# First weight piece of an LN-MLP kernel moved to ACT's DMA queue, and three more filling products

## The chip, the cores and the metric

One core of one Trainium2 chip. The time is the device time of one execution in microseconds (us). Three runs of the kernel before gave 396.5, 396.9 and 397.19 us; the median is 396.9.

## The reference

```
y = _layernorm(x, axis=-1)                                    # x: 1 x 2048 x 1024, no scale or shift
h = gelu(einsum("bsd,df->bsf", y, w1) + b1, approximate=True) # w1: 1024 x 3584
return einsum("bsf,fd->bsd", h, w2) + b2                      # w2: 3584 x 1024
```

All tensors are bf16.

## The kernel before, in words

The 2048 rows of x are cut into 16 tiles of 128 rows (tile 0 to tile 15), and these into 4 blocks of 512. For each block the first GEMM makes h (28 rows of 128 features, each a sum over 8 slices `dt` of the 1024 inputs), ACT applies bias and gelu from PSUM, and the second GEMM makes the output, to which DVE adds b2. The instruction order of each engine is written out by hand: every operation is put on a list of its engine (`sp`, `pe`, `act`, `dve`, `pool`) with the names of the events it waits for, and the lists are emitted in that order. Every load of the kernel before is on SP's list.

The opening is about block 0, where x and w1 are still on their way. What the prediction's steps touch:

- **Loads** (`dma`, L185 to 186; `LOADS`, L32; issued at L208 to 226). SP issues x tile 0 (x0), x tile 1 (x1), then w1 in pieces: c0, c1, c2, then b1, c3, c4, x tile 2 (x2), c5 and so on. A piece cN of the first sixteen is one slice `dt` of w1 for 8 rows: 128 x 1024 bf16, 256 KB, as large as an x tile. c0 to c3 are dt 0 to 3 of rows 0 to 7, c4 to c7 the same dt of rows 8 to 15, c8 to c15 dt 4 to 7 of the same rows; c16 and on serve rows 16 to 23 and the last ones.
- **Filling products** (`fill`, L295; called at L542 and L544). A matmul of ones into a bank that is overwritten later. Nine of 512 columns stand at the head of PE's list; then come two transposes of tile 0, two filling products of 128 columns, and two transposes of tile 1.
- **Centring.** For tiles 0 and 1 ACT and DVE each sum a part of the row (L431 and L434), DVE subtracts the mean (L440, result in c_sb), PE transposes slices of c_sb against an identity matrix (`pe_T`, L311), and ACT copies the transposed slices to yT_sb (L317). Scaling by 1/std comes later, on the products (below).
- **The order of products** (`OPEN`, L23; `pe_cell`, L339): slice 0 with c0 for tile 0 (8 products of 128 columns), four transposes, slice 0 with c0 for tile 1 (8 more), then slices 1 to 3 with c1 to c3 for both tiles (8 products of 256 columns for each piece), then c4 to c7, c8 to c15, c16 and on. Two rows share a PSUM bank (a unit). The eight banks are full after unit 7, so unit 8 (row 16) needs bank 0 and unit 9 (row 18) needs bank 1 again; each is free when ACT's gelus of that bank's first unit are done (L380).
- **What frees those banks.** After x2 has landed, DVE takes its mean (L478), moves slices of tiles 0 and 1 (L494), normalises and transposes tile 2 (L484, L487), spreads the factors 1/std (L519 to L530), and multiplies the products of the first units by them (L370). ACT's gelus of these units (L380) come behind that.

SP and PE list, as code:

```
LOADS = (0, 1, 2, "b1", 3, 4, -2, 5, 6, 7, 8, 9, 10, -3) + tuple(range(11, 22))
...
        fill(N_FILL_A, TPB)
        pe_T(0, GROUPS[0][0], c_sb[:, 0, :])
        fill(N_FILL_C, 1)
        pe_t[0] = T_PE_START
```

Of the kernel before, what the change touches and what calls it, by code (L numbers as in the profile page):

```python
# [11 lines left out]
P = 128  # L12
TB = 512
TPB = TB // P
# [2 lines left out]
UGROUPS = ((0, 4), (4, 8), (8, 10), (10, 11), (11, 12))  # L17
NPAIR = 2 * UGROUPS[-1][1]
NCEN = 2
N_FILL_A = 9  # L20
N_FILL_C = 2
JT = 4
OPEN = (("T", 1, 0), (0, 0, 1, 0, 1), ("T", 0, 1), ("T", 1, 1), (0, 1, 2, 0, 1), (0, 0, 2, 1, JT), (1, 0, 2, 0, JT),  # L23
        (0, 0, 2, JT, 8), (1, 0, 2, JT, 8), (2, 0, 2, 0, 8), (3, 0, 2, 0, 8), (4, 0, 2, 0, 8))
# [4 lines left out]
          ((0, 2, 6), (2, JT, 4)))  # L29
ACT_BLOCKS_01 = ((0, 1), (0, 2), (1, 2), (1, 3))  # L30
ACT_BLOCKS = ((0, 1), (0, 2), (0, 3), (1, 2), (1, 3), (2, 3))
LOADS = (0, 1, 2, "b1", 3, 4, -2, 5, 6, 7, 8, 9, 10, -3) + tuple(range(11, 22))  # L32
NOB = 2
TAIL_CUTS = (0, 384, 512)
N_W2_CHUNKS = 2
# [58 lines left out]
def bass_standalone__mixer_channel_mlp__prompt_kernel(  # L94
# [46 lines left out]
    w1v = w1.rearrange("(t p) f -> p t f", p=P)  # L141
    w2v = w2.rearrange("(t p) d -> p t d", p=P)

    with ExitStack() as es:
        sb = lambda name, shape, dt: es.enter_context(nc.sbuf_tensor(name, shape, dt))

        w1_sb = sb("w1_sb", [P, DT, F], BF16)
# [22 lines left out]
        ps = es.enter_context(nc.psum_tensor("ps", [P, NBANK, 512], F32))  # L170
        psb = ps[:, :, :].bitcast(BF16)
        one = nc.const_aps.tensor(1.0, [P, P], BF16)

        sp = _Prog(None)
        pe = _Prog("s_pe")
        act = _Prog("s_act")
# [8 lines left out]
        def dma(dst, src, sig, nbytes, q=None):  # L185
            (q or sp).op(lambda e, dst=dst, src=src: e.dma_start(dst, src), sig=sig, sem="d_" + sig, inc=16)  # L186
            dma_bytes[0] += nbytes
            est[sig] = DMA_T0 + dma_bytes[0] / DMA_BYTES_PER_US

        def load_x_tile(i, q=None):  # L190
            dma(x_sb[:, i, :], xf[i * P:(i + 1) * P, :], f"x{i}", P * D * 2, q)
            x_ev[i] = f"x{i}"
# [4 lines left out]
            for i in range(b0 * TPB, b1 * TPB):  # L197
                x_ev[i] = f"xb{b0}"

        def load_w1(ci):  # L200
            j0, j1, a, b = w1_chunks[ci]
            dma(w1_sb[:, j0:j1, a:b], w1v[:, j0:j1, a:b], f"w1c{ci}", (j1 - j0) * P * (b - a) * 2)

        def load_w2(ci):
            dma(w2_sb[:, ci * W2C:(ci + 1) * W2C, :], w2v[:, ci * W2C:(ci + 1) * W2C, :], f"w2c{ci}",
# [2 lines left out]
        for i in range(2):  # L208
            load_x_tile(i)
        for o in LOADS:  # L210
            if o == "b1":
                sp.op(None, waits=["b1z"])
                dma(b1r_sb[0:FT, :], b1.rearrange("(t p) -> t p", p=P), "b1", F * 2)
            elif o < 0:
                load_x_tile(-o)
            else:
                load_w1(o)
        assert n_open == 1 + max(o for o in LOADS if o != "b1")
        for ci in range(n_open, len(w1_chunks)):
            load_w1(ci)  # L220
# [4 lines left out]
        if NB > 2:  # L225
# [4 lines left out]
                sig="ident")  # L230
# [61 lines left out]
        bank_read = {}  # L292
        pe_t = [T_PE_START]

        def fill(n, k):  # L295
            rhs = one.unsqueeze(1).broadcast_to([P, k, P])
            for _ in range(n):
                pe.op(lambda e: e.matmul(ps[:, 0, 0:k * P], lhsT=one, rhs=rhs, start=True, stop=True))  # L298

        def pe_T(i, group, src):  # L300
            blk, t = divmod(i, TPB)
            j0, j1, bank = group
            bap = psb[:, bank, :]
            evs = yT_ev.setdefault(i, [None] * DT)
            for j in range(j0, j1):
                waits = []
                if j == j0:
                    waits = ["ident"] + ([bank_read[bank]] if bank in bank_read else [])
                if j == j0 or y_ev[i][j] != y_ev[i][j - 1]:
                    waits.append(y_ev[i][j])  # L310
                pe.op(lambda e, j=j, o=(j - j0) * P: e.transpose(  # L311
                    out=bap[:, o:o + P], in_=src[:, j * P:(j + 1) * P], identity=ident[:, :]),
                    waits=waits, sig=(f"tp{i}_{j0}" if j == j1 - 1 else None))
                evs[j] = f"te{i}_{j0}"
            psrc = bap[:, 0:(j1 - j0) * P].rearrange("p (j s) -> p j s", j=j1 - j0)
            dst = yT_sb[:, blk % 2, j0:j1, t * P:(t + 1) * P]
            act.op(lambda e, dst=dst, psrc=psrc: e.copy(out=dst, in_=psrc), waits=[f"tp{i}_{j0}"], sig=f"te{i}_{j0}")  # L317
            bank_read[bank] = f"te{i}_{j0}"
            pe_t[0] += (j1 - j0) * 0.056
# [106 lines left out]
            store_last[(ob, region)] = sev  # L426

        act.op(lambda e: e.preload_act_table(ACT.Gelu_apprx_tanh))
        def sums(i, na):
            n2 = (D - na) // 2  # L430
            act.op(lambda e: e.activation(out=hT_sb[:, 2 * NRAW + i, 0:na], in_=x_sb[:, i, 0:na], func=ACT.Copy,  # L431
                                          scale=1.0 / D, accum_out=sum_sb[:, 2 * i:2 * i + 1]),
                   waits=[f"x{i}"], sig=f"sa{i}")
            return (lambda e: e.tensor_tensor_reduce(out=o_sb[:, i, 0:n2], in0=x_sb[:, i, na:na + n2],  # L434
                                                     in1=x_sb[:, i, na + n2:D], op0=ALU.add, op1=ALU.add,
                                                     scale=1.0 / D, scalar=0.0, accum_out=sum_sb[:, 2 * i + 1:2 * i + 2]),
                    [f"x{i}"], f"sd{i}")

        def centre(i, j0, j1):
# [4 lines left out]
            y_ev.setdefault(i, []).extend([f"y{i}_{j0}"] * (j1 - j0))  # L444

        sd = [sums(0, SA0), sums(1, HC)]
        def turn_half(i):
            dve_put((lambda e: e.transpose(out=hT_sb[:, NPAIR - 4 + i, :], in_=c_sb[:, i, JT * P:D]), y_ev[i][JT:DT],
# [10 lines left out]
        for i in range(NCEN):  # L459
            pool.op(lambda e, i=i: e.tensor_tensor(out=tot_sb[:, i:i + 1], in0=sum_sb[:, 2 * i:2 * i + 1],  # L460
                                                   in1=sum_sb[:, 2 * i + 1:2 * i + 2], op=ALU.add),
                    waits=[f"sa{i}", f"sd{i}"], sig=f"tot{i}")
# [60 lines left out]
        for q in range(4):  # L523
            f = q ^ 1
# [3 lines left out]
        for h in range(2):  # L528
            f = h ^ 1
# [7 lines left out]
        for k, (tq, q) in enumerate(joint):  # L537
            if k == 4:
                dve_put(op_rm_pair(N_RM_EARLY - 1, N_RM_EARLY - 1))
            move(dve, 2, 2, tq, q)  # L540

        fill(N_FILL_A, TPB)  # L542
        pe_T(0, GROUPS[0][0], c_sb[:, 0, :])
        fill(N_FILL_C, 1)  # L544
        pe_t[0] = T_PE_START

# [80 lines left out]
        ci = fi = 0  # L627
        while ci < len(crit) or fi < len(fills):
            take_crit = fi >= len(fills)
            if not take_crit and ci < len(crit):  # L630
                rel_f, _, blk_f = fills[fi]
                if crit[ci][0] <= max(t_dve, rel_f) + CRIT_SLACK and blk_f > crit[ci][2]:
                    take_crit = True
            if take_crit:
                rdy, o, _ = crit[ci]
                ci += 1
            else:
                rdy, o, _ = fills[fi]
# [46 lines left out]
```

## Time and profile before

| | before |
|---|---|
| three runs, us | 396.5, 396.9, 397.19 (median 396.9) |
| the profiled execution, us | 396.88 |
| span of its instructions, us | 395.6 |
| PE busy | 392.7 us of the span, 99% |
| PE from 0 to 5 us, and from 5 to 10 us | busy 4.17 and 4.77 us |
| DMA, first 30 us | 342 GB/s on the mean |
| granted TensorE clock over the span | 1.0 |

The span begins with the first instruction and ends with the last; 1.28 us of the profiled execution's time lie outside it. In a row of the timeline the columns are the start in us, the length in us, the engine, the line, the operation, what it writes and reads, how many instructions are merged in the row, and in brackets the idle time of the engine before it and what ended that. PE is TensorE's matmul, PEld its weight load (each matmul has one), SPq is SP issuing a DMA. Matmul records overlap, since a record runs to the end of the pipeline; the distance from start to start is the rate. A DMA has landed when all its parts have been reported to its semaphore.

### The profile page before, as it was taken

Reading aid. Unit: us, or ns where it says so; the run is one execution under the profiler, and the core shown is the slowest. Engines: PE = TensorE matmul, PEld = TensorE weight load, DVE = VectorE, ACT = ScalarE, POOL = GpSimd, SP = SyncE. Lnnn points to the kernel's source line nnn. Section 1 sums busy time; section 2 is a strip of 40 time slices with the busy share of each in tenths; the row PEclk is TensorE's granted clock in tenths of the full one; section 3 lists DMA queues with packets and bytes.
Section 4 is the critical chain, followed back from the end, with each engine's and each line's share of the span. In section 5 each row is a group of like instructions: output and inputs, shape, how many; then the busy total and the mean of one; then the engine's idle time right before and its main releaser. Section 6 shows DMA issues by size and latency. Waiting matters only on the chain.

```text
span 395.6 us, 4775 instructions
## 1 busy us (share of the span) xinstructions
PE 392.7 (99%) x2039; PEld 197.6 (50%) x2039; DVE 155.6 (39%) x344; ACT 94.4 (24%) x169; POOL 10.8 (3%) x31
## 2 busy tenths in 40 slices
PE   8999999999999999999999999999999999999998
PEld 5888844444444444444444444444444444444445
DVE  5998989989996005987100000001100000001011
ACT  6787520000144332000023443100003334400000
POOL 1202000110002000000000000000000000000000
DMA  8999940000000000000000000000000000000000
GB/s 284 377 366 384 386 148 22 17 29 13 27 2 0 0 2 0 29 23 17 28 13 0 2 0 0 15 13 27 25 16 15 0 0 2 0 13 28 13 27 28
DMA packets 16190, 23.64 MB, mean 60 GB/s; under 512 B 1194, under 2 KB 8362, under 8 KB 16170
## 3 DMA queue, kind: packets, MB, share of 16 engines
q1 hardware_dynamic: 16170, 23.34, 16.7%
q8 instruction: 16, 0.26, 0.3%
q14 instruction: 4, 0.03, 0.0%
HBM read 19.14 MB, written 4.19 MB: 59 GB/s over the span
## 4 chain that ended last, share of the span: by engine, by line
PE 98%; DMA 1%; SPq 0%; DVE 0%; issue 0%
PE ps L408 49%; PE ps L339 49%; DMA w_sb<-in_w_dram 1%; SPq L186 0%; DVE o_sb L419 0%
## 5 line engine op out<-in xcount | busy, mean ns | idle before, releaser
L339 PE MATMUL ps<-yT_sb,w_sb 128*128 128x512 bf16 (+2 forms) x1096 | 195.0, 340 | 0.1
L408 PE MATMUL ps<-w_sb,hT_sb 128*128 128x512 bf16 (+2 forms) x924 | 194.1, 373 | 0.0
L339 PEld LDWEIGHTS ps<-yT_sb,w_sb 128*128 128x128 bf16 x1096 | 106.3, 98 | 87.8 <-DMA w_sb<-in_w_dram 0.3
L408 PEld LDWEIGHTS ps<-w_sb,hT_sb 128*128 128x128 bf16 x924 | 89.3, 98 | 104.5
L359 ACT ACTIVATE hT_sb<-ps,b_sb 128x512 bf16<-128x512 f32 x88 | 60.5, 688 | 236.3 <-PE ps L339 231.9
L419 DVE TENSOR_TENSOR o_sb<-ps,b_sb 128x512 bf16<-128x512 f32 (+2 forms) x33 | 22.3, 675 | 198.3 <-PE ps L408 198.3
L284 DVE STREAM_TRANSPOSE yT_sb<-x_sb 32x256 bf16<-32x256 bf16 x192 | 83.7, 436 | 28.8 <-PE ps L339 25.8
L380 ACT ACTIVATE hT_sb<-ps,b_sb 128x256 bf16<-128x256 f32 x48 | 18.8, 507 | 8.6 <-PE ps L339 7.3
L237 DVE BATCH_NORM_STATS2 st_sb<-x_sb 128x6 f32<-128x512 bf16 x24 | 15.8, 667 | 0.1
L242 POOL TENSOR_TENSOR rstd_sb<-mv_sb,nhalf 128x1 f32<-128x1 f32 x12 | 6.6, 548 | 100.4 <-DVE mv_sb L245 100.4
L252 DVE TENSOR_SCALAR x_sb<-x_sb,mv_sb,rstd_sb 128x1024 bf16<-128x1024 bf16 x12 | 6.6, 546 | 3.0 <-POOL rstd_sb L242 2.0
L370 DVE TENSOR_TENSOR ps<-ps,rbc_sb 128x512 f32<-128x512 f32 x12 | 7.5, 693 | 0.1
L503 ACT COPY yT_sb<-o_sb 32x256 bf16<-32x256 bf16 x12 | 4.8, 402 | 3.1 <-DVE o_sb L487 2.9
L298 PE MATMUL ps<-const-bfloat16-1.0 128*128 128x512 bf16 (+1 forms) x11 | 4.4, 568 | 0.8 <-PEq L670 0.8
L245 DVE BATCH_NORM_AGGREGATE mv_sb<-st_sb 128x2 f32<-128x15 f32 x12 | 2.7, 223 | 1.2
L503 DVE COPY yT_sb<-o_sb 32x512 bf16<-32x512 bf16 x10 | 2.8, 284 | 0.2
L298 PEld LDWEIGHTS ps<-const-bfloat16-1.0 128*128 128x128 bf16 x11 | 1.4, 139 | 2.7 <-issue 2.7
L494 DVE COPY yT_sb<-hT_sb 32x256 bf16<-32x256 bf16 x12 | 2.6, 218 | 0.1
L487 DVE STREAM_TRANSPOSE o_sb<-c_sb 128x1024 bf16<-128x1024 bf16 x2 | 2.5, 1245 | 0.1
L466 ACT ACTIVATE hT_sb<-x_sb,sum_sb 128x1024 bf16<-128x1024 bf16 x2 | 2.3, 1148 | 0.6 <-DVE sum_sb L478 0.6
L466 ACT ACTIVATE hT_sb<-x_sb,tot_sb 128x1024 bf16<-128x1024 bf16 x2 | 2.3, 1146 | 0.0
L434 DVE CUSTOM_DVE_ANT_0 o_sb<-x_sb 128x384 bf16<-128x384 bf16 (+1 forms) x2 | 1.0, 488 | 3.3 <-DMA x_sb<-in_x_dram 3.3
(33 smaller groups left out, 23.4 us busy)
## 6 DMA issues: line engine op xcount, KB each, us to landing
w_sb<-in_w_dram SPq DMA_DIRECT2D x2, 3584.0 KB, 22.2
w_sb<-in_w_dram SPq DMA_DIRECT2D x18, 256.0 KB, 5.7
out_dram<-o_sb SPq DMA_DIRECT2D x31, 128.0 KB, 1.7
x_sb<-in_x_dram SPq DMA_DIRECT2D x1, 2048.0 KB, 17.1
w_sb<-in_w_dram SPq DMA_DIRECT2D x3, 512.0 KB, 9.9
x_sb<-in_x_dram SPq DMA_DIRECT2D x4, 256.0 KB, 4.0
w_sb<-in_w_dram SPq DMA_DIRECT2D x1, 1024.0 KB, 10.2
x_sb<-in_x_dram SPq DMA_DIRECT2D x1, 1024.0 KB, 11.4
```

Of the source, the lines that this page charges most:

```text
L237: return (lambda e, i=i, h=h: e.bn_stats(st_sb[:, i, 6 * h:6 * (h + 1)], x_sb[:, i, h * HC:(h + 1) * HC]), [x_ev.get(i, f"x{i}_{h}")], f"s ...
L242: pool.op(lambda e, i=i, to=to: e.tensor_tensor(out=to[:, i:i + 1], in0=mv_sb[:, i, 1:2], in1=nhalf[:, i:i + 1], op=ALU.pow), waits=[f"mv{ ...
L252: return (lambda e, i=i: e.tensor_scalar(out=x_sb[:, i, :], in0=x_sb[:, i, :], scalar1=mv_sb[:, i, 0:1], scalar2=rstd_sb[:, i:i + 1], op0= ...
L284: res.append((lambda e, src=src, dst=dst: e.transpose(out=dst, in_=src), waits, (f"tr{i}" if lastop else None), 0.47))
L298: pe.op(lambda e: e.matmul(ps[:, 0, 0:k * P], lhsT=one, rhs=rhs, start=True, stop=True))
L339: pe.op(lambda e, dt=dt: e.matmul(ps[:, bank, o0:o0 + n1 - n0], lhsT=w1_sb[:, dt, r * P:(r + 1) * P], rhs=yT_sb[:, b % 2, dt, n0:n1], star ...
L359: act.op(lambda e, r=r, bank=bank: e.activation(out=hT_sb[:, r, :], in_=ps[:, bank, :], func=ACT.Gelu_apprx_tanh, bias=b1_sb[:, r:r + 1], ...
L370: return (lambda e: e.tensor_tensor(out=pv, in0=pv, in1=rv, op=ALU.mult), [f"mp0_{u}", "rbc"], f"rmp_{u}", 0.70)
L380: act.op(lambda e, r=r, k=k: e.activation(out=hT_sb[:, r, half * NC:(half + 1) * NC], in_=ps[:, bank, k * NC:(k + 1) * NC], func=ACT.Gelu_ ...
L408: pe.op(lambda e, st=st, ft=ft, c0=c0, c1=c1, bank=bank: e.matmul(ps[:, bank, 0:c1 - c0], lhsT=hT_sb[:, ft, st * P:(st + 1) * P], rhs=w2_s ...
L419: crit.append((est[sig], (lambda e, ob=ob, c0=c0, c1=c1, bank=bank: e.tensor_tensor(out=o_sb[:, ob, c0:c1], in0=ps[:, bank, 0:c1 - c0], in ...
L503: op = (lambda e: e.tensor_copy(out=dst, in_=src)) if eng is dve else (lambda e: e.copy(out=dst, in_=src))
```

## The change

c0 is taken off SP's list. ACT issues it on its own DMA queue, after it has loaded its function table and has waited until the fourth of the nine filling products is done; on ACT's list this stands ahead of the sums of tiles 0 and 1. The nine filling products are issued in the same place as before (4 and 5, the fourth now signals). The filling products between tile 0's and tile 1's transposes are five instead of two. Nothing else moves: PE's, DVE's and POOL's lists are otherwise the same, and SP's list is the same without c0.

```diff
-N_FILL_A = 9
-N_FILL_C = 2
+N_FILL_A = (4, 5)
+N_FILL_C = 5
...
-LOADS = (0, 1, 2, "b1", 3, 4, -2, 5, 6, 7, 8, 9, 10, -3) + tuple(range(11, 22))
+ACT_LOADS = (0,)
+LOADS = (1, 2, "b1", 3, 4, -2, 5, 6, 7, 8, 9, 10, -3) + tuple(range(11, 22))
...
-        def load_w1(ci):
+        def load_w1(ci, q=None):
             j0, j1, a, b = w1_chunks[ci]
-            dma(w1_sb[:, j0:j1, a:b], w1v[:, j0:j1, a:b], f"w1c{ci}", (j1 - j0) * P * (b - a) * 2)
+            dma(w1_sb[:, j0:j1, a:b], w1v[:, j0:j1, a:b], f"w1c{ci}", (j1 - j0) * P * (b - a) * 2, q)
...
-        def fill(n, k):
+        def fill(n, k, sig=None):
             rhs = one.unsqueeze(1).broadcast_to([P, k, P])
-            for _ in range(n):
-                pe.op(lambda e: e.matmul(ps[:, 0, 0:k * P], lhsT=one, rhs=rhs, start=True, stop=True))
+            for i in range(n):
+                pe.op(lambda e: e.matmul(ps[:, 0, 0:k * P], lhsT=one, rhs=rhs, start=True, stop=True),
+                      sig=sig if i == n - 1 else None)
...
         act.op(lambda e: e.preload_act_table(ACT.Gelu_apprx_tanh))
+        act.op(None, waits=["fill"])
+        for ci in ACT_LOADS:
+            load_w1(ci, act)
...
-        fill(N_FILL_A, TPB)
+        fill(N_FILL_A[0], TPB, "fill")
+        fill(N_FILL_A[1], TPB)
         pe_T(0, GROUPS[0][0], c_sb[:, 0, :])
         fill(N_FILL_C, 1)
```

## The prediction, as put on record before the changed kernel ran

> **What bounds the kernel now.** I read the page first: PE is the bound, and the change can only move the few microseconds in which PE is not.
>
> ```profile
> PE 392.7 (99%) x2039; PEld 197.6 (50%) x2039; DVE 155.6 (39%) x344; ACT 94.4 (24%) x169; POOL 10.8 (3%) x31
> ```
>
> Then the chain that ended last, over the first 20 us. From 6.95 us on it is matmuls alone; ahead of them stands one load, whose issue began at 2.16 and which landed at 6.91. That is c1, SP's fourth.
>
> ```profile
> 2.16 4.75 DMA w_sb<-in_w_dram
> 6.91 0.04 issue
> 6.95 13.09 PE ps L339 x118
> ```
>
> Third, the timeline of the weight loads from 4.1 to 7.2 us, because their brackets name what PE waited for.
>
> ```profile
> 4.45 0.32 PEld L311 LDWEIGHTS ps<-ident,c_sb 128*128 128x128 bf16 x2 [0.53 <-POOL tot_sb L460]
> 4.72 0.25 PEld L298 LDWEIGHTS ps<-const-bfloat16-1.0 128*128 128x128 bf16 x2
> 5.39 0.11 PEld L311 LDWEIGHTS ps<-ident,c_sb 128*128 128x128 bf16 x2 [0.41 <-DVE c_sb L440]
> 5.56 0.46 PEld L339 LDWEIGHTS ps<-yT_sb,w_sb 128*128 128x128 bf16 x8
> 5.98 0.27 PEld L311 LDWEIGHTS ps<-ident,c_sb 128*128 128x128 bf16 x4
> 6.20 0.49 PEld L339 LDWEIGHTS ps<-yT_sb,w_sb 128*128 128x128 bf16 x8
> 6.95 0.33 PEld L339 LDWEIGHTS ps<-yT_sb,w_sb 128*128 128x128 bf16 x4 [0.26 <-DMA w_sb<-in_w_dram]
> ```
>
> The transposes of tile 1 wait for its centring until 5.39. The first product's weights load at 5.56, its matmul starts at 5.59. The 16 small products and 4 transposes end at 6.70; then PE stands for 0.25 us until c1 is there.
>
> Last I looked for the next place where PE stands. There is one, near 20.4 us, and its cause is not a load:
>
> ```profile
> 20.42 0.66 PEld L339 LDWEIGHTS ps<-yT_sb,w_sb 128*128 128x128 bf16 x7 [0.23 <-ACT hT_sb L380]
> ```
>
> From 20.20 to the next start at 20.43 the matmuls lose 0.12 us (0.227 against their usual 0.109): unit 9 waits for bank 1, that is, for ACT's gelus. What these wait for is read from DVE's and ACT's timelines:
>
> ```profile
> 9.63 0.69 DVE L478 CUSTOM_DVE_ANT_0 o_sb<-x_sb 128x512 bf16<-128x512 bf16 x1 [0.74 <-DMA x_sb<-in_x_dram]
> ...
> 18.07 1.90 DVE L370 TENSOR_TENSOR ps<-ps,rbc_sb 128x512 f32<-128x512 f32 x3
> ```
>
> ```profile
> 18.80 2.30 ACT L380 ACTIVATE hT_sb<-ps,b_sb 128x256 bf16<-128x256 f32 x6
> ```
>
> DVE starts when x2 lands (9.61) and works to 18.07 and beyond with no gap over 0.11 us. So the release of bank 1 at 20.37 hangs on the landing of x2, not on PE's start. This decides the forecast: whatever PE gains before 20.4 it waits away there, unless x2 lands earlier too; and of what PE loses, the first 0.12 us cost nothing.
>
> **The change part by part.**
>
> *SP without c0.* An issue takes 0.42 us, and the next starts 0.47 us later. c1 goes from 2.16 to 1.69, into c0's old place, and everything behind it moves up by 0.47: c2, b1 (its other wait, POOL's clearing of its tile, is over at 1.32), c3, c4, x2 (4.48 to 4.01). I expect c1 some tenths earlier than 6.91, between c0's old landing (1.69 + 3.6 = 5.3) and c1's own, and the 0.25 us wait gone. I do not expect x2 earlier. Issues come every 0.47 us, but c2, c3, c4, x2 and c5 land at 7.57, 8.23, 8.89, 9.61 and 10.24, about 0.66 apart: here the transfers set the pace, and by 9.6 us the same bytes must be through, c0 among them. The gain from this part is 0.25 us at 6.95 and nothing at 20.4. [...]
>
> *c0 on ACT's queue.* The fourth fill starts at 2.06 and its record ends 0.63 later, at 2.69; ACT's table load is over at 2.06. ACT can issue at about 2.73 instead of SP's 1.69. An issue costs 0.35 to 0.46 us in SP's rows; the trace shows none on ACT, and I take the same, so until 3.15. Behind it on ACT's list stand the sums of tile 0, which wait for x0:
>
> ```profile
> 3.30 0.42 ACT L431 ACTIVATE hT_sb<-x_sb 128x256 bf16<-128x256 bf16 x1 [1.24 <-DMA x_sb<-in_x_dram]
> ```
>
> x0 lands at 3.28, so the issue is hidden by 0.13 us; a longer one delays tile 0's centring, which has 0.17 us more (weights ready 4.45, PE busy with the ninth fill until 4.62). Tile 1's sums start at 4.17, well after.
>
> When does c0 land? PE needs it at 5.53. The rows of 256 KB loads, from issue to landing: x0 2.5 us (nothing ahead), x1 2.9 (one load ahead), c0 itself 3.6 (two ahead), c1 4.7 (three ahead). From 2.73 these give 5.2, 5.65, 6.4 and 7.5. The last is excluded: by 6.91 the kernel before had moved x0, x1, c0 and c1 whole, and the new order asks for no more bytes by then, so 6.91 is my upper end and 5.2 the lower. I take x1's row, 5.65: c0's own queue is empty, and sharing the engines with an equal load is like having one ahead. Then the first product starts at 5.69 instead of 5.59, the small ones end at 6.80, and c1 is there: PE enters the 256-column products 0.15 us earlier than at 6.95. In general PE's shift there is (landing + 0.04 + 1.11) - 6.95, that is landing - 5.80; with the 0.12 us of slack at 20.4 the end of the kernel moves only if c0 lands after 5.92.
>
> It may also take turns with x1's last parts, which land from 3.71 to 4.14. Doubling what is left at 3.74 costs tile 1's chain at most 0.4 us: products from 5.99 instead of 5.59, 7.10 instead of 6.95, 0.03 over the slack.
>
> *Three more fills.* The two now start at 4.83 and 4.94, 0.107 apart. Five end at 4.83 + 5 x 0.107 = 5.37, and tile 1's transposes cannot start before 5.39. They lie in the wait for centring and cost nothing; were centring done at once, they would cost 0.32.
>
> *Sum.* -0.25 at 6.95, +0.10 for c0, and at 20.4 the remaining -0.15 goes into the wait for bank 1 (0.12 becomes 0.27). Zero on the end: 396.88 + 0 = 396.9 us, for the profiled execution as for the median of the runs, from which it differs by 0.02. A measurement of this kernel can tell about 0.2%, 0.8 us, from no change.
>
> **The rivals.**
>
> *Slower: c0 comes with the last DMA engines.* The parts of one load do not land together: 14 parts of c1 are there by 6.01, the last two at 6.66 and 6.91. If c0 shares those two engines with c1 until both are through, it lands near 6.9. Then products start at 6.95, the small ones end at 8.06, 1.11 late; less 0.12 of slack: +0.99, 397.9 us. It decides above 0.2% from a landing of 6.7. For it: this lag is in every later load as well. Against it: x0 and x1 show only 0.2 to 0.4 of it. Chance 0.18. In between, c0's own 3.6 us gives 6.4 and +0.45, 397.3 us: chance 0.17, not told from no change.
>
> *Faster: x2 lands earlier.* In the stretch from 4.25 to 5 us the engines moved only 229 to 320 GB/s against 390 later, so some transfer time is unused; a second queue may fill it. If x2 gains the 0.47 us of its issue, PE keeps its 0.25 and the 0.12 at bank 1: -0.37, 396.5 us. Chance 0.13, mostly inside 0.2%.
>
> *The fills change the clock.* Matmuls of 128 columns come 107 ns apart at 4.8 us and 55 ns apart at 5.6, so the step lies in the idle stretch that the fills take. If in unprofiled runs the stretch delays the step past 6.70, the fills save 20 x 0.052 = 1.0 us: 395.9 us. Against it: the profiled execution, with the step in time, stands at the runs' median. Chance 0.04. [...]
>
> **How the numbers follow.** No change on the end 0.48; c0 moderately late 0.17; with the last engines 0.18; x2 earlier 0.13; the clock 0.04. Over +0.2%: 0.18 and some of the moderate case, 0.22 in all. Below -0.2%: the clock and a little of x2, 0.06. The range goes from 396.4 (x2 early, and the lowest run shown is 396.5) to 397.9, the upper end of c0's landing.
>
> **What would show it.** Right: c0 issued on ACT near 2.7 and landed between 5.2 and 5.9; no wait for c1 near 6.9; x2 within 0.2 of 9.61; the wait at 20.4 longer than 0.23. Wrong: the first product after 6, with a load named in its bracket; ACT's first sum after 3.4; a bank wait that ends before 20.2.

## The result, and the profile after

Six executions of the changed kernel took 397.99 to 401.84 us, median 400.38; the kernel before, beside it, 396.50 to 397.19, median 396.78. The ratio is 1.0082, with an interval of 1.0055 to 1.0109: slower by 0.8%. Two more sessions gave 1.0052 (1.0027 to 1.0077) and 1.0077 (1.0060 to 1.0094). The forecast was 396.9, at most 397.9.

The profiled execution took 398.73 us with a span of 397.5, so 1.9 us more span than before. On the page, PE is as busy as before, and a second DMA queue has appeared: q10 is ACT's, with c0's 0.26 MB.

```profile
PE 392.8 (99%) x2042; PEld 198.0 (50%) x2042; DVE 155.5 (39%) x344; ACT 94.4 (24%) x169; POOL 10.9 (3%) x31
...
q10 hardware_dynamic: 144, 0.26, 0.2%
```

The chain over the first 20 us now runs through ACT's load: four filling products, the issue at 2.73, and 5.12 us to the landing of c0 at 7.84.

```profile
0.78 0.04 issue
0.83 1.88 PE ps L299 x4
2.71 0.02 issue
2.73 5.12 DMA w_sb<-in_w_dram
7.84 0.05 issue
7.89 0.62 PE ps L341 x8
...
```

The weight loads from 4.1 to 9.3 us, the answer to the list that the prediction shows:

```profile
4.65 0.14 PEld L313 LDWEIGHTS ps<-ident,c_sb 128*128 128x128 bf16 x2 [0.73 <-POOL tot_sb L465]
4.74 0.58 PEld L299 LDWEIGHTS ps<-const-bfloat16-1.0 128*128 128x128 bf16 x5
5.45 0.13 PEld L313 LDWEIGHTS ps<-ident,c_sb 128*128 128x128 bf16 x2
7.89 0.45 PEld L341 LDWEIGHTS ps<-yT_sb,w_sb 128*128 128x128 bf16 x8 [2.31 <-DMA w_sb<-in_w_dram]
8.29 0.27 PEld L313 LDWEIGHTS ps<-ident,c_sb 128*128 128x128 bf16 x4
8.52 0.82 PEld L341 LDWEIGHTS ps<-yT_sb,w_sb 128*128 128x128 bf16 x12
```

The five fills end just ahead of tile 1's transposes (5.45), as forecast. Then PE stands for 2.31 us, and the bracket names the load. When the 256-column products begin at 9.02 (6.95 before), c1 has been there since 6.46, so the old wait for it is gone, and so is the wait for bank 1 near 20.4. PE comes there 2.07 us later. The gelus that free the bank are later as well, but only by 1.34 us: they began at 18.80 before. ACT's rows from 9 to 24 us, cut:

```profile
9.19 1.16 ACT L471 ACTIVATE hT_sb<-x_sb,tot_sb 128x1024 bf16<-128x1024 bf16 x1
...
12.13 1.15 ACT L471 ACTIVATE hT_sb<-x_sb,sum_sb 128x1024 bf16<-128x1024 bf16 x1
...
20.14 2.29 ACT L382 ACTIVATE hT_sb<-ps,b_sb 128x256 bf16<-128x256 f32 x6
```

ACT's issue took 0.37 us, where SP's up to 5 us took 0.35 to 0.46 in the kernel before, and delayed nothing. ACT's first sum starts 0.02 us behind x0, which landed at 3.48 in this execution.

```profile
2.73 0.37 ACTq L187 DMA_DIRECT2D w_sb<-in_w_dram  x1
3.50 0.42 ACT L436 ACTIVATE hT_sb<-x_sb 128x256 bf16<-128x256 bf16 x1 [1.44 <-DMA x_sb<-in_x_dram]
```

The late landing explains the profiled execution to a tenth: by the prediction's own formula, a landing at 7.84 costs 7.84 - 5.92 = 1.92 us, and the span grew by 1.9. It does not explain the median. The executions lie in steps, by the mean granted TensorE clock of each. Over the changed kernel's 19 executions in three sessions (one more is left out, below):

| granted clock | executions | us, lowest / median / highest |
|---|---|---|
| 1.0 | 9 | 397.91 / 398.47 / 399.50 |
| 0.996 | 7 | 399.69 / 400.29 / 401.21 |
| 0.991 | 3 | 401.65 / 401.71 / 401.84 |

A share of 0.004 of 399 us is 1.6 us lost, 0.009 is 3.6. So there are two losses: by the medians, about 1.6 us because c0 is late, and in about half of the executions 1.8 or 3.2 us more at a lowered clock. Both profiled executions of the changed kernel (this one and that of e7) are at 1.0; the fall itself is read from variants of it below.

### The profile page after: what moved, and what is told of

It reads as the page before. It is cut to its first block, busy times and chain, and to the rows that moved or that the text cites. A ratio compares the mean times of both kernels' runs of the same rounds, so it can differ in the third digit from the quotient of the medians.

```text
span 397.5 us, 4781 instructions
## 1 busy us (share of the span) xinstructions
PE 392.8 (99%) x2042; PEld 198.0 (50%) x2042; DVE 155.5 (39%) x344; ACT 94.4 (24%) x169; POOL 10.9 (3%) x31
## 3 DMA queue, kind: packets, MB, share of 16 engines
HBM read 19.14 MB, written 4.19 MB: 59 GB/s over the span
## 4 chain that ended last, share of the span: by engine, by line
PE 98%; DMA 1%; DVE 0%; issue 0%
PE ps L341 49%; PE ps L410 49%; DMA w_sb<-in_w_dram 1%; PE ps L299 0%; DVE o_sb L421 0%; PE ps L313 0%
## 5 line engine op out<-in xcount | busy, mean ns | idle before, releaser
L358 DVE TENSOR_TENSOR ps<-ps,rbc_sb 128x256 f32<-128x256 f32 x4 | 1.7, 433 | 1.8 <-PE ps L341 1.8
L471 ACT ACTIVATE hT_sb<-x_sb,sum_sb 128x1024 bf16<-128x1024 bf16 x2 | 2.3, 1148 | 0.0
```

## The experiments

Theory A, order: a load lands by how many were issued ahead of it, on whichever queue. Theory B, queue: ACT's queue is slow by itself, or two queues at work together are. Theory C: PE, standing for c0, loses its clock. e1 to e4 ran on one chip, e5 and e6 on a second, e7 to e9 together, e10 and e11 together, e12 alone, e13 and e14 together.

**e1_fills_only**: c0 back on SP, the five fills kept.

```diff
-ACT_LOADS = (0,)
-LOADS = (1, 2, "b1", 3, 4, -2, 5, 6, 7, 8, 9, 10, -3) + tuple(range(11, 22))
+ACT_LOADS = ()
+LOADS = (0, 1, 2, "b1", 3, 4, -2, 5, 6, 7, 8, 9, 10, -3) + tuple(range(11, 22))
...
-        act.op(None, waits=["fill"])
```

> c0 back in its old place on SP's list, no wait and no load on ACT; only the three extra filling products of the change are kept. Theory A (c0's late landing is the whole loss, the fills cost nothing): 396.8 us, ratio 0.999 to 1.001, granted clock 1.0 in every run. Rival (the fills or the fuller array disturb the clock): the granted clock falls below 1.0 in some runs and the time goes to 398 us or more.

Measured: 396.54 to 397.75, median 397.12, ratio 0.9998 (0.9984 to 1.0011), clock 1.0 in all ten. The fills cost nothing; all of the loss is in c0.

**e2_sp_late**: no load on ACT; c0 on SP behind c1, c2 and b1.

```diff
-ACT_LOADS = (0,)
-LOADS = (1, 2, "b1", 3, 4, -2, 5, 6, 7, 8, 9, 10, -3) + tuple(range(11, 22))
+ACT_LOADS = ()
+LOADS = (1, 2, "b1", 0, 3, 4, -2, 5, 6, 7, 8, 9, 10, -3) + tuple(range(11, 22))
...
-        act.op(None, waits=["fill"])
```

> No load on ACT; c0 stands on SP's list behind x0, x1, c1, c2 and b1, that is, at the place in time at which ACT issued it (about 2.7 to 3.1 us). Theory A, order (a load lands by how many were issued ahead of it, whichever queue it is on): c0 lands at 7.5 to 8.0 us as in the changed kernel, time 398 to 402 us, with the granted clock under 1.0 in some runs. Theory B, queue (ACT's queue itself starts late or is served slowly): c0 lands by 7 us or earlier and the time is within 1 us of the kernel before.

Measured: median 398.33, ratio 1.0042 (1.0024 to 1.0061), clock 0.996 in 4 of 10. c0, issued at 3.15, landed at 6.95; PE stood for it 0.85 us:

```profile
6.04 0.11 PEld L313 LDWEIGHTS ps<-ident,c_sb 128*128 128x128 bf16 x2 [0.39 <-DVE c_sb L444]
6.99 0.45 PEld L341 LDWEIGHTS ps<-yT_sb,w_sb 128*128 128x128 bf16 x8 [0.85 <-DMA w_sb<-in_w_dram]
```

The place alone, on SP's queue, gives a loss of the same kind. It looks smaller than the changed kernel's (398.0 against 398.5 us at full clock, by the medians of six and nine executions), but the intervals of the ratios overlap. The forecasts split: the landing, 6.95, is theory B's (by 7 us) and misses theory A's 7.5; the time, 1.4 us above the kernel before, and the lowered clock are theory A's.

**e3_act_first**: ACT issues c0 with no wait, ahead of its table load.

```diff
-        act.op(lambda e: e.preload_act_table(ACT.Gelu_apprx_tanh))
-        act.op(None, waits=["fill"])
         for ci in ACT_LOADS:
             load_w1(ci, act)
+        act.op(lambda e: e.preload_act_table(ACT.Gelu_apprx_tanh))
```

> c0 on ACT's queue, but with no wait and ahead of the function table's load, so issued at about 0.8 us, beside x0. Theory A, order: c0 is then the second load and lands between 3.5 and 4.5 us; x1 lands some tenths later than 4.14 because c0 is ahead of it; time 396.5 to 397.3 us, clock 1.0. Theory B, queue: c0 still lands over 4.5 us after its issue (5.3 us or later), and the time rises if that is past 5.9 us.

Measured: c0, issued at 0.78, landed at 4.64, a little later than forecast; but x0 landed at 4.45 (3.28 before) and x1 at 5.14 (4.14 before). Median 397.85, ratio 1.0026 (1.0011 to 1.0042). c0 is not late here; with it beside x0, x0 is late, which the forecast had left out, and the transposes of tile 0 start at 5.66 instead of 4.62, the microsecond that the time shows.

**e4_bridge**: the changed kernel, with 40 fills in the stretch in which PE stands.

```diff
                 pe_T(t, GROUPS[t][g], c_sb[:, t, :])
+                if (t, g) == (1, 0):
+                    fill(40, 1)
```

> The changed kernel with 40 more filling products of 128 columns between tile 1's first transposes and the first product, that is, in the 2.3 us in which PE stands for c0. They take 2.2 us at 56 ns each, and up to 4.3 us at 107 ns. Theory C (beside the direct wait of about 1.9 us, the standing PE loses its clock in two of three executions, worth 1.6 to 3.6 us): granted clock 1.0 in every run and all times within 1 us of each other, 398 to 399 us. Rival (the clock falls for another cause than the standing PE): clocks under 1.0 and times up to 401.8 us stay.

Measured: 398.79 to 399.29 in nine executions, median 399.01, clock 1.0 in all nine. c0 landed at 7.45, but the fills held PE until 8.11, which is why it is not faster still.

```profile
5.47 2.68 PEld L299 LDWEIGHTS ps<-const-bfloat16-1.0 128*128 128x128 bf16 x40
8.11 0.49 PEld L341 LDWEIGHTS ps<-yT_sb,w_sb 128*128 128x128 bf16 x8
```

Nine of nine at full clock and a spread of 0.5 us, against 9 of 19 and 3.9 us without the bridge: theory C holds. The changed kernel did not run beside it; e2, which did and in which PE stands too, had 4 of 10 at 0.996.

**e5_sp_held**: the changed kernel, but SP holds c1 and all behind it until the ninth fill is done.

```diff
                 else:
+                    if o == 1:
+                        sp.op(None, waits=["fill9"])
                     load_w1(o)
...
-        fill(N_FILL_A[1], TPB)
+        fill(N_FILL_A[1], TPB, "fill9")
```

> The changed kernel, but SP holds c1 and everything behind it until the ninth filling product is done (4.8 us instead of 1.7), so that c0 on ACT's queue has only x0 and x1 ahead of it and nothing beside it. The time is of no interest (all later loads come 3 us late). Theory A, order: c0 is the third load and lands 2.5 to 3.6 us after its issue at 2.73, at 5.2 to 6.3 us. Theory B, a second queue that starts late whatever SP does: its first data come at 4.9 us again and it lands 4.5 us or more after its issue, past 7 us. If it lands at about 6 us the two share the blame.

Measured (one execution, 399.34 us): c0, issued at 2.73 on ACT's queue as in the changed kernel, landed 2.7 us later, at 5.40, where the changed kernel's took 5.1.

```profile
L187 ACTq DMA_DIRECT2D w_sb<-in_w_dram x1: 372/372/372, 2.7 to 2.7; - x1
...
DMA to landing us min/median/max: 2.7/2.7/2.7
```

ACT's queue is not slow by itself: with c1 and all behind it held back, 2.7 us from issue to landing. By this pair c0 waits in the changed kernel for what SP has in flight. When c0's data begin to move shows the same: by then SP's queue had moved 0.52 MB, that is x0 and x1, at 3.73 in e5; 0.83 MB, over three loads, at 4.90 in the changed kernel, where two of c0's 144 packets came earlier.

**e6_x1_act**: w1 all on SP; x1 on ACT, ahead of the table load.

```diff
-ACT_LOADS = (0,)
-LOADS = (1, 2, "b1", 3, 4, -2, 5, 6, 7, 8, 9, 10, -3) + tuple(range(11, 22))
+ACT_LOADS = ()
+LOADS = (0, 1, 2, "b1", 3, 4, -2, 5, 6, 7, 8, 9, 10, -3) + tuple(range(11, 22))
...
-        for i in range(2):
+        load_x_tile(0)
+        load_x_tile(1, act)
+        for i in range(0):
             load_x_tile(i)
...
-        act.op(None, waits=["fill"])
```

> All w1 pieces on SP as in the kernel before; instead x1 goes to ACT's queue, issued at about 0.8 us beside x0, ahead of the function table's load; five fills as in the change. c0 and all behind it move up by 0.47 us on SP's list. Theory A, order: x1 is second as before, c0 third, c1 fourth; the issue times are earlier, so c1 lands by 0.1 to 0.4 us earlier and x1 by up to 0.4; time 396.3 to 396.9 us, since the bank wait at 20.4 us takes back what PE gains unless x2 lands earlier. Theory B, a slow second queue: x1 lands after 5 us, tile 1's centring is late by a microsecond, time 397.5 us or more.

Measured: median 397.06 (396.95 to 397.24), ratio 0.9992 (0.9976 to 1.0008): no change. x0 landed at 4.19, x1 at 4.39, c0 at 4.87. As in e3, x0 is late with a load beside it, and the first product starts at 6.35 (5.59 before). Why the median does not show that stays open. Theory B's forecast fails; theory A's time is missed by 0.2 us, and its x1, which it had earlier, came 0.25 later.

**e7_after_again**: the changed kernel once more.

> The changed kernel once more, to see more executions and, if the profiled one has it, the place at which the clock falls. Order and clock theories together: c0 lands at 7.3 to 7.9 us; executions come in steps by their granted clock, about 398.3 us at 1.0, 1.7 us more at 0.996 (one window of about 3.4 us at half rate) and 3.4 us more at 0.991 (two). If the clock is not tied to PE standing for c0, the half rate lies elsewhere in the span than in the first 20 us.

Measured: 397.91 to 401.71, median 398.75, ratio 1.0052 (1.0027 to 1.0077); clock 1.0 in seven, 0.996 in two, 0.991 in one. c0 landed at 8.09 in the profiled execution, 0.2 past the range. That execution is at 1.0; a stretch of 3.4 us at half rate stands in the traces of e10 (7.26 to 10.68) and e12 (8.51 to 11.93), two of them in none.

**e8_fill1**: ACT waits for the first fill. **e11_fill1_again**: the same once more.

```diff
-N_FILL_A = (4, 5)
+N_FILL_A = (1, 8)
```

> The changed kernel, but ACT waits for the first filling product instead of the fourth, so it issues c0 right after its table load, at about 2.1 us instead of 2.73. Order theory: c0 is then issued ahead of c2 (2.16) or level with it, one load earlier, and lands 0.5 to 0.9 us earlier than in the changed kernel (6.6 to 7.2 us); the time lies between the kernel before and the changed one, 397.3 to 398.3 us at full clock. Rival (what counts is that c0 is on the second queue, not when it is issued): it lands at 7.3 us or later as before and the time stays at 398 to 402 us.

> The version in which ACT waits for the first filling product only, once more and with more rounds, to see whether it beats the kernel before (first time: ratio 0.9992, interval 0.998 to 1.0003). If the earlier landing of x2 (8.45 against 9.61 us) lets PE keep what it waited at 6.95 and 20.4 us, the gain is 0.25 + 0.12 = 0.37 us, ratio 0.999, and the interval lies below 1. If the bank wait or the start of the clock takes it back: ratio 0.9995 to 1.0005, not told from no change.

Measured: median 396.93, ratio 0.9992 (0.998 to 1.0003), and 396.82, ratio 0.9997 (0.9984 to 1.0009); clock 1.0 in all 21. ACT issued at 1.44, not at 2.1: the table load (0.78 to 2.06) did not hold up the issue. So c0 went ahead of c1 (1.70) and landed third, at 4.83 and 4.98, outside both forecasts of e8. x2 came at 8.45 and 8.35. The loss is gone, and a gain over the kernel before is not told from no change.

**e9_two_fills**: c0 on ACT as in the change, two fills.

```diff
-N_FILL_C = 5
+N_FILL_C = 2
```

> The other half of the change alone: c0 on ACT's queue as in the changed kernel, but two filling products between the transposes as in the kernel before. Theory (the fills neither cost nor save): the same as the changed kernel, 398 to 402 us, with the clock under 1.0 in about two of three executions. Rival (the fills make the clock rise earlier, so that the standing PE then loses it): fewer executions with a clock under 1.0 and a median under 399 us.

Measured: median 399.29, ratio 1.0048 (1.0024 to 1.0072): the loss of e7 again, so it belongs to c0 alone. Three of ten were at 0.996, not two thirds, but a mean of 1.0 is no proof of a full clock here: another of the ten took 401.43 us at 1.0. A late start is seen in the profiled execution, whose mean is 1.0 as well: its first eight products take 1.04 us (0.62 in the changed kernel), 107 ns apart, and its trace has the clock stepping up at 9.97 us. Of the rival's forecast, fewer executions under 1.0 came out, a median under 399 did not.

```profile
6.90 1.04 PE L341 MATMUL ps<-yT_sb,w_sb 128*128 128x128 bf16 x8 [0.70 <-DMA w_sb<-in_w_dram]
```

**e10_fill2**: ACT waits for the second fill. **e12_fill2_again**: the same once more.

```diff
-N_FILL_A = (4, 5)
+N_FILL_A = (2, 7)
```

> The changed kernel, but ACT waits for the second filling product, whose record ends at 1.84 us, so it issues c0 at about 1.87: after c1 (1.69) and ahead of c2 (2.16). Order theory: c0 is the fourth 256 KB load, between the first-fill version (third, landed 4.83) and the changed kernel (fifth, landed 7.8): 5.5 to 6.9 us. PE's small products then start 0 to 1.2 us late; time 397.0 to 398.2 us. Rival (only the queue counts): as in the changed kernel, landing at 7.3 us or later, 398 us or more.

> The version that waits for the second filling product once more; the first time c0, issued at 1.87, landed at 7.34 with the engines at 219 and 299 GB/s from 4 to 6 us (against 379 and 365 in the version that waits for the first). If that was the chance of one execution (slow first transfers of w1) and order decides: c0 lands at 5.5 to 6.9 us with more than 300 GB/s in that stretch, and the times scatter between 396.8 and 399.8 us. If a load on ACT's queue beside a load on SP's is itself slow: it lands past 7 us again, and all executions are near 399.7 us.

Measured: 399.62 to 399.78 in four executions, ratio 1.0070 (1.0057 to 1.0084), then 398.10 to 400.28 in six, ratio 1.0051 (1.0024 to 1.0079). c0, issued at 1.87, landed at 7.34 and 7.58; c1, issued ahead of it at 1.70 on SP, at 7.15 and 7.40. Theory A's 5.5 to 6.9 is wrong twice, so order is not all. The forecast that all executions of e12 are near 399.7 failed as well: two of the six, 398.10 and 398.58, were at full clock.

```profile
7.38 0.77 PEld L341 LDWEIGHTS ps<-yT_sb,w_sb 128*128 128x128 bf16 x8 [1.97 <-DMA w_sb<-in_w_dram]
```

These profiled executions also show the clock fall; the rows are those of e10. The columns are the stretch, its length, PE, PEld, DVE, ACT and POOL busy, PEclk, the DMA share and GB/s:

```profile
5.00:6.00 1.00, 0.38 (x4) 0.11 (x2) 0.97 (x3) 0.58 (x2) 0.07 (x1) 1.00 0.87 299
6.00:7.00 1.00, 0.00 (x0) 0.00 (x0) 0.97 (x3) 0.00 (x0) 0.00 (x0) 1.00 1.03 299
7.00:8.00 1.00, 0.62 (x7) 0.62 (x8) 0.44 (x2) 0.00 (x0) 0.00 (x0) 0.63 0.96 355
8.00:9.00 1.00, 1.00 (x12) 1.00 (x11) 0.87 (x5) 0.33 (x2) 0.00 (x0) 0.50 1.05 389
9.00:10.00 1.00, 1.00 (x10) 0.88 (x9) 0.28 (x2) 1.00 (x3) 0.00 (x0) 0.50 1.04 383
10.00:11.00 1.00, 1.00 (x8) 0.77 (x7) 0.97 (x5) 0.96 (x4) 0.38 (x2) 0.66 1.06 408
11.00:12.00 1.00, 1.00 (x11) 0.90 (x10) 0.95 (x5) 0.98 (x3) 0.38 (x1) 1.00 1.04 399
```

PE does nothing from 6 to 7 us; in e10 the clock is full from 3.85 to 7.26 and half from 7.26 to 10.68, just as PE has work again. The lost shares, 0.37 + 0.50 + 0.50 + 0.34, make 1.71 us, near the table's 1.8. With the landing by the formula, 7.34 - 5.92 = 1.42, that is 3.1 us; the span grew by 2.9. In e12 the clock is half from 8.51 to 11.93, and the same sum gives 3.4 for 3.3.

**e13_sp_fourth**: no load on ACT; c0 fourth on SP's list, the place that e10 gave it.

```diff
-ACT_LOADS = (0,)
-LOADS = (1, 2, "b1", 3, 4, -2, 5, 6, 7, 8, 9, 10, -3) + tuple(range(11, 22))
+ACT_LOADS = ()
+LOADS = (1, 0, 2, "b1", 3, 4, -2, 5, 6, 7, 8, 9, 10, -3) + tuple(range(11, 22))
...
-        act.op(None, waits=["fill"])
```

> No load on ACT; c0 is the fourth 256 KB load on SP's list, behind x0, x1 and c1 (issued at 2.16), so it has the place it had on ACT's queue in the version that waits for the second filling product (issued at 1.87, landed at 7.34 and 7.58). If the place alone sets the landing, it lands past 7 us here too, near c1, and the time is 399 us or more. If two queues at work at once add to it, c1 lands at 5.0 to 5.7 us, c0 at 5.7 to 6.9, and the time is 396.8 to 398.2 us.

Measured: median 397.18, ratio 1.0017 (0.9998 to 1.0035), clock 0.996 in two of ten. c1 landed at 5.23, c0 at 5.87; PE stood for c0 for 0.48 us. Against e10 and e12, c0 in the same place is 1.5 to 1.7 us earlier on one queue than on two, and c1, third in all three, 1.9 to 2.2 us. The three ran on three chips.

```profile
5.91 0.45 PEld L341 LDWEIGHTS ps<-yT_sb,w_sb 128*128 128x128 bf16 x8 [0.48 <-DMA w_sb<-in_w_dram]
```

**e14_after_third**: the changed kernel beside e13.

> The changed kernel a third time, beside the one before on the same chip, to set its two-queue transfers against SP's alone in one session. Place and queue together: c0 lands at 6.8 to 8.1 us, 219 to 312 GB/s from 4 to 5 us, 398 to 402 us in steps of the clock. Place alone: the landing and the rate from 4 to 6 us do not differ from the version with c0 on SP by more than the one load that is ahead (0.7 us).

Measured: 399.69, 400.03 and 400.04 us, all at 0.996, ratio 1.0077 (1.0060 to 1.0094). Its profiled execution ran with matmuls of 512 columns 840 ns apart all through (1486 us) and is left out, so the rates that it was to give came from the other profiles:

| where c0 stands | c0 lands, us | GB/s, 4 to 5 and 5 to 6 us |
|---|---|---|
| third, SP (before; e1) | 5.32; 5.39 | 264, 349; 324, 352 |
| third, ACT (e8; e11) | 4.83; 4.98 | 379, 365; 406, 403 |
| fourth, SP (e13) | 5.87 | 381, 346 |
| fourth, ACT (e10; e12) | 7.34; 7.58 | 219, 299; 215, 260 |
| fifth, SP (e2) | 6.95 | 404, 398 |
| fifth, ACT (changed; e4; e7; e9) | 7.84; 7.45; 8.09; 6.85 | 231, 322; 303, 324; 267, 330; 312, 376 |

Each entry is one execution. Other 256 KB loads on SP, in traces with no load on ACT, widen the rows: the fourth landed at 6.91 (c1, before), 6.14 (e1) and 6.07 (e2), the fifth at 7.57 (c2, before), 6.77 (e1) and 6.55 (e13). So the fourth place on ACT, 7.34 and 7.58, lies beyond all of SP's, but the fifth, 6.85 to 8.09, overlaps with SP's 6.55 to 7.57: for the changed kernel itself the place explains most of the delay, and a further cost of the second queue is not told from the scatter of c0's landing.

The clearest sign of such a cost is the third load, which is issued at 1.7 behind x0 and x1. With all loads on SP it landed at 5.23 to 5.39 (before, e1, e2, e13). With c0 following on ACT it was c1, and it landed at 6.46 to 7.40 in five executions (changed, e7, e9, e10, e12) and at 5.12 in one (e4). The rates go the same way, but not as clearly: 264 GB/s from 4 to 5 us stand in the kernel before, on one queue.

## Why the prediction was wrong, step by step

**SP without c0** was right for c1, which landed at 6.46. x2 missed by a little: 9.32 is 0.29 earlier than 9.61, forecast within 0.2. Its reason, that the transfers set the pace and the same bytes must be through, does not hold: in e8 and e11 x2 landed at 8.45 and 8.35 with the same bytes. The faster rival had that right. **ACT's issue** was right: 2.73 to 3.10, hidden. **The three fills** were right: e1 shows no cost. **The formula** from landing to end was right to 0.1 us at full clock: 1.92 for 1.9 here, 2.17 for 2.1 in e7, 1.03 for 1.0 in e2, and none for -0.1 in e13. **Where the gain goes** was never put to the test by the change itself, since PE came late; in e8 both waits were gone and the time still did not leave the noise. That the release of bank 1 hangs on x2 and not on PE's start is wrong for a late PE: here x2 came 0.29 us earlier, yet the gelus began 1.34 us later. ACT first has to copy the late transposes, so it squares tile 0 (L471) at 9.19 instead of 6.88, and tile 2, behind it in its list, at 12.13 instead of 10.36. DVE then waits for tile 2's factor 1/std, which POOL makes from these squares:

```profile
14.40 0.55 DVE L489 TENSOR_SCALAR c_sb<-x_sb,sum_sb,rs_sb 128x1024 bf16<-128x1024 bf16 x1 [1.68 <-POOL rs_sb L478]
```

The 0.12 us of slack counted all the same, as PE came later still.

**The landing of c0 was the step that failed.** The prediction took x1's row, 2.9 us, since "c0's own queue is empty, and sharing the engines with an equal load is like having one ahead". Measured: 5.1. The row that fitted was in the trace of before: c2, issued at 2.63, 0.1 us from ACT's issue, took 4.9 and landed at 7.57; from 2.73 its row gives 7.67. c2 there and c0 here both had four 256 KB loads ahead of them. Its own empty queue did not lift c0 over what SP's had in flight: in the changed kernel's trace q10 has 2.7% of the engines' time from 2.8 to 4.8 us, and q1 92.8%; from 4.8 to 6.3 the two queues share it nearly evenly:

```profile
q1 hardware_dynamic: 174, 0.27, 52.0%
q10 hardware_dynamic: 119, 0.22, 45.6%
```

Why c0 got almost nothing in the 2 us before, with c1 and c2 under way, no run shows.

The reason that excluded the upper row failed as well. "The new order asks for no more bytes by then" counted x0, x1, c0 and c1, but c2 was issued ahead of c0 too. And the slower rival, the nearest to what happened, put c0 with the last engines at 6.9; even its end lay a microsecond short.

**The clock** was in the forecast only as a gain from the fills. It was a second loss. PE's wait was priced as time, 1 us for 1 us; in e10 it also cost 1.71 us, one stretch at half rate, and in e4, where fills kept PE busy, all nine executions stayed at 1.0. In e10 this stretch, 7.26 to 10.68, is 3.41 us long. Ahead of it PE stood for 1.79 us, and its matmul records cover 1.40 of the 3.41 us from 3.85 to 7.26.

The other traces allow a comparison. Their clock records come in steps of 3.413 us: the stretch at half rate is one step, and the changed kernel's at full rate, 392.53 us, is 115 of them. In the first step after the clock had gone up, the matmul records cover 1.40 us in e10 and 1.52 in e12, and the clock fell. They cover 1.79 in e7, 1.85 in the changed kernel's profiled execution, 1.89 in e3 and 2.5 or more in the others that record a clock, and it stayed. That the executions at 0.996 are those in which most of PE's stand fell into one such step would fit this, but it is the author's estimate: none of the changed kernel's at 0.996 was profiled.

**What stays open:** why c0 third on ACT (issued at 1.44) is harmless while fourth (1.87) is not, and why c1 lands a microsecond or more later with c0 behind it on ACT. Whether the 0.991 executions hold two such steps at half rate was not seen in a trace; twice 1.71 us would fit the table's 3.2.

## What to carry to other kernels

In this kernel a second queue was no fast lane: c0 took 5.12 us on it, where the forecast had 2.9 (x1's row). Price a moved load by the row that was issued at the same time (c2's 4.9 us here), not by the row with an empty queue, and count every load in flight on the other queue. Where the first product hangs on the load, put its issue ahead of the loads it would otherwise wait for (issued at 1.44 in e8, c0 landed at 4.83), though not beside the very first one (issued at 0.78 in e3, it landed at 4.64, but x0 only at 4.45), or leave it where it is. A stand of PE in the opening can be paid twice, as in e10, where c0 came 1.42 us late and the clock took 1.71 us more; look at the granted clock of every execution, and fill a stand that can't be avoided, with no more than it lasts (in e4 the 40 fills ran 0.66 us past c0's landing).

## What had not been expected of the hardware

- A load issued together with x0 at the start went with a later x0: x0 landed at 4.45 (e3) and 4.19 (e6) beside another load, at 3.28 to 3.63 in the others but e2 (4.07, with none beside it).
- ACT's table load (1.28 us) did not hold up a DMA on ACT's queue: in e8 it was issued at 1.44, in the middle of it.
- The clock stepped up at quite different times: in the traces that record it, between 3.73 (e3) and 9.97 us (e9) after the start. Five traces (before, e6, e8, e11, e14) hold no such record and have a mean of 1.0 all the same. Of the kernel before, 7 of the 105 executions beside the experiments took 398.8 to 399.5 us: two (399.40 and 399.52) at a mean clock of 0.996, five at 1.0. Whether a late step lies behind the five no trace shows.
- Among the 41 executions that keep the five fills and have c0 or x1 early (e1, e6, e8, e11) none was over 397.8. That the fills guard against a late clock is suggested by this, not shown.
